# Parking part of Wq between the rows of a zero tile, and moving half of the backward stores to another queue

## The chip, the cores and the metric

The kernel runs on one core of a Trainium2 chip. A core has a matrix engine (TensorE, PE in the profile; PEld is its weight load), VectorE (DVE), ScalarE (ACT), GpSimd (POOL) and SyncE (SP). Transfers between the chip's memory and the on-chip buffer (SBUF, 128 partitions) are issued from SP, POOL or ACT and are carried out by 16 DMA engines. The metric is the device time of one execution in microseconds, as the median of several runs.

## The reference, cut to what matters

One token (448 numbers) goes through a pre-norm attention layer over a sliding window of 4096 cached keys and values, and through a gated bilinear layer. The function returns the output and the gradients of every input but one:

```python
    W = min(4096, max(256, Sk // 4))            # 4096 of Sk = 32768
    q = (x @ wq).reshape(B, Sq, Hq, Dh)...      # 16 heads of 256
    k = jnp.repeat(k_cache[:, :, Sk - W:, :], rep, axis=1)
    v = jnp.repeat(v_cache[:, :, Sk - W:, :], rep, axis=1)
    p = _softmax(jnp.einsum("bhqd,bhkd->bhqk", q, k) * (Dh ** -0.5), axis=-1)
    o = jnp.einsum("bhqk,bhkd->bhqd", p, v)
...
    h = x + _A_ref(_layernorm(x), ...)
    h2 = h + _B_ref(_layernorm(h), ...)
    _out, _vjp = jax.vjp(_f, A_x, A_k_cache, A_v_cache, A_wq, A_wo, B_w_gate, B_w_up, B_w_down)
    return (_out, *_vjp(grad_out))
```

The gradients of the two caches (`out_2` for K, `out_3` for V) have the caches' full shape, 8 heads x 32768 x 256 in bf16. Only the last 4096 positions of each head are computed; the other 28672 are zeros that the kernel must write: 16 regions of 14.7 MB each. Together with the rest the kernel writes 280.6 MB and reads 49.2 MB.

## The kernel before

**Zeros.** The tile `zeros` has 128 partitions of 8192 bf16 numbers (16 KB each). Partitions 32 to 95 are set to zero at the start. A fill (`fill`, L81) reads 16 of them, every fourth from 32 to 92 (`ALL`), again and again into a region of `out_2` or `out_3`. SP's queue (`FILL`) issues 15 whole regions and part of the last one, one after the other (L86 to L104). What is left of the last region is dealt out in small pieces on POOL's queue (`deal_rest`, `lap` 0 in the middle and `lap` 1 at the very end), some partitions with more than others. Partitions 0 to 31 and 96 to 127 of `zeros` hold something else from the forward pass on: quarters of the moments (`quarter`, L124). The 48 partitions between the fills' rows (33 to 35, 37 to 39 and so on) are zero and are read by nothing.

**Wq.** The weight of 448 x 4096 is laid out as 128 partitions of 14336 numbers: seven blocks of `HQ` = 2048, called i = 0 to 6. It is loaded twice. At the start SP loads all but the first `KW` = 896 columns into the big buffer `BIG` (L68), and ScalarE's queue loads those 896 into a place where they stay (`wq_kept`, L69). The buffer's slots are then used for V. For the gradient of x, in the backward loop, POOL loads Wq again (`dxn_load`, L653, blocks 0 to 3 after step 2 and 4 to 6 after step 3 of the loop) and VectorE multiplies each block with dq and sums it up (`wq_product`, L657; `dxn_part`, L661).

**Forward.** q is made by 112 small matmuls (L306). Then, for each of the 8 heads of K and V, PE transposes K (L341), forms the scores, VectorE scales K by the softmax (L394) and PE forms moments (L398 to L404). POOL's queue (`IO`) loads K, V and all later weights in an order that is written out by hand (`io_load`, each issued after the one before). A feed-forward part with its own gradients follows.

**Backward loop.** Eight steps s (L757), one for each head. In each, 32 matmuls (L764) make the rows of the gradients of K and V, which ScalarE and VectorE copy in turn out of PSUM into a pair of slots of `BIG` (`evac`, L289). When a step's 32 rows are there, POOL's queue stores the two halves of the pair, 2 MB each (L788). Which slots a step uses stands in `PAIR`; a slot can be written again when its store has landed. VectorE also works at jobs for the other gradients in between (`during`, L693: `o4_job` to `o8_job` are outer products that are stored from POOL's queue, `dxn_part` the second use of Wq, `dx_out` the gradient of x).

Waits between engines are semaphores that the tile framework sets. It has eight for transfers issued from SP and ACT together, used in turn, and eight for those from POOL; a transfer that takes a semaphore waits until the transfer that had it eight before has landed.

Of the kernel before, what the change touches and what calls it, by code (L numbers as in the profile page):

```python
# [42 lines left out]
def kernel(  # L43
# [23 lines left out]
    for c0, c1 in ((KW, 4 * HQ), (4 * HQ, NI * HQ)):  # L67
        FILL.dma_start(out=wq_sb[:, c0:c1], in_=flat_rows(A_wq)[:, c0:c1])  # L68
    S_.dma_start(out=wq_kept, in_=flat_rows(A_wq)[:, 0:KW])  # L69
# [4 lines left out]

    zeros = const.tile([128, ZW], bf16)
    for p in (32, 64):
        V_.memset(zeros[p:p + 32, :], 0.0)
    def region(o, g):
        return o[0, g, 0:Sk - W, :].rearrange("s d -> (s d)")

    def fill(eng, flat, rows, n, f):  # L81
        p = len(range(128)[rows])
        eng.dma_start(out=flat.rearrange("(p n f) -> p n f", p=p, f=f), in_=zeros[rows, 0:f].unsqueeze(1).to_broadcast([p, n, f]))

    ALL = slice(32, 93, 4)
    for g in range(G):  # L86
        for o in (out_2, out_3):
            if (g, o) != (G - 1, out_3):
                fill(FILL, region(o, g), ALL, 8 * NZ, ZW)
# [12 lines left out]
    deal(FILL, 0, 3, 14)  # L102
    deal_all(24, ZW)
    deal_all(8, 1224)  # L104
# [68 lines left out]


# [4 lines left out]
    ones_f = const.tile([128, 128], f32)  # L179
    V_.memset(ones_f[:], 1.0)  # L180
# [106 lines left out]
    evac_ctr = [0]  # L287

    def evac(out, in_):  # L289
        if evac_ctr[0] % 2 == 0:  # L290
            S_.copy(out=out, in_=in_)  # L291
        else:
            V_.tensor_copy(out=out, in_=in_)  # L293
# [10 lines left out]
    for b in range(16):  # L304
        for i in range(NI):
            P_.matmul(q_ps[:, :, b], lhsT=wq_at(i, b * 128, 128), rhs=xx1[:, i, :], start=(i == 0), stop=(i == NI - 1))  # L306
# [341 lines left out]
    wq2 = [slot(3 + i // 4)[:, (i % 4) * HQ:(i % 4 + 1) * HQ] for i in range(NI)]  # L648

    def wq_from(i):  # L650
        return 0 if i else KW

    def dxn_load(i0, i1):  # L653
        c = wq_from(i0)
        IO.dma_start(out=slot(3 + i0 // 4)[:, c:(i1 - i0) * HQ], in_=flat_rows(A_wq)[:, i0 * HQ + c:i1 * HQ])

    def wq_product(w, i, c, n):  # L657
        V_.tensor_tensor_reduce(out=w, in0=w, in1=dq_bc[:, i % 2, c:HQ] if c else dq_bc[:, i % 2, 0:w.shape[-1]], scale=1.0, scalar=0.0,  # L658
                                op0=ALU.mult, op1=ALU.add, accum_out=Pq[:, n:n + 1])

    def dxn_part(i0, i1):  # L661
        if i0 == 0:
            wq_product(wq_kept, 0, 0, NI)
            yield
        for i in range(i0, i1):
# [156 lines left out]
```

## Time and profile before

| | us |
|---|---|
| median of 3 runs (778.31 to 779.84) | 778.7 |
| the profiled execution | 779.32 |
| its span, first to last instruction | 777.5 |
| DVE busy in the span | 402.0 (52%) |
| PE busy | 468.0 (60%) |
| ACT busy | 177.1 (23%) |
| POOL busy | 43.3 (6%) |

The span is what the views of the trace divide into stretches; the profiled execution's own time is 1.8 us longer. Of the 330.4 MB that were moved, SP's queue (q1) moved 230.9 MB, POOL's (q0) 98.6 MB and ScalarE's (q10) 0.2 MB. A row of the costliest groups names line, engine, operation and tiles, then the busy time and the mean of one in ns, then the idle time before and what ended it. A row of DMA issues names tiles, queue and count, the size of one in KB and the median time from issue to landing. The chain of waits is followed back from the last instruction.

### The profile page before, as it was taken

The numbers are of one execution on the slowest core, as the hardware profiler recorded it, in microseconds if no ns is written. First come the engines' busy times: TensorE is split into PE (matmuls) and PEld (weight loads), VectorE is DVE, ScalarE is ACT, GpSimd is POOL, SyncE is SP. The second block draws the span as 40 slices with busy tenths as digits, with TensorE's granted clock in tenths as the row PEclk, the third lists the DMA queues.
The fourth block names the chain that finished last, engine by engine and source line by source line (L and its number), as shares of the span: only waits on it lengthen the run. The fifth ranks groups of instructions, "written<-read, shape, count | busy, mean of one in ns | idle before, by whom it ended". The sixth has DMA issues, their size and how long they took to land.

```text
span 777.5 us, 10855 instructions
## 1 busy us (share of the span) xinstructions
PE 468.0 (60%) x4375; PEld 257.5 (33%) x4420; DVE 402.0 (52%) x1179; ACT 177.1 (23%) x278; POOL 43.3 (6%) x88
## 2 busy tenths in 40 slices
PE   4798898899899612234076998980957598200000
PEld 3654554565555311113052443430333232000000
DVE  5477677677667311255954656667577377200000
ACT  0322322321120000034333444440413244100000
POOL 3000000000000000010000001000001010100000
PEclk9998998999999855555555555555555555555555
DMA  9999999999999999999999999999999999999998
GB/s 363 427 425 428 426 425 430 428 426 428 424 428 429 429 430 430 433 430 430 424 428 430 430 429 430 428 427 431 428 430 429 429 427 431 430 433 432 428 429 349
DMA packets 25683, 330.44 MB, mean 425 GB/s; under 512 B 3069, under 2 KB 3199, under 8 KB 5046
## 3 DMA queue, kind: packets, MB, share of 16 engines
q1 hardware_dynamic: 14557, 230.94, 69.6%
q0 software_dynamic: 10928, 98.59, 30.1%
q8 instruction: 34, 0.56, 0.3%
q10 hardware_dynamic: 148, 0.23, 0.1%
q14 instruction: 16, 0.12, 0.0%
HBM read 49.15 MB, written 280.59 MB: 424 GB/s over the span
## 4 chain that ended last, share of the span: by engine, by line
PE 40%; DMA 28%; DVE 13%; issue 4%; ACT 2%; another core or an unknown queue 2%; POOL 0%; POOLq 0%; DVEq 0%; ACTq 0%
PE MT L398 12%; DMA out_dram<-BIG 10%; PE tr L341 8%; PE d_ps L764 7%; DMA BIG<-in_B_w_down_dram 7%; DMA BIG<-in_A_wq_dram 6%; DMA BIG<-in_A_k_cache_dram 4%; DVE BIG L588 2%; PE sT L346 2%; DMA BIG<-in_A_wo_dram 2%; DVE BIG L574 1%; PE dp L346 1%; DVE zeros L415 1%; ACT BIG L291 1%
## 5 line engine op out<-in xcount | busy, mean ns | idle before, releaser
L764 PE MATMUL d_ps<-BIG 32*128 32x512 bf16 x256 | 121.8, 607 | 41.3 <-ACT BIG L291 23.9
L398 PE MATMUL MT<-BIG 128*128 128x512 bf16 x467 | 140.4, 409 | 2.1 <-DVE BIG L394 0.4
L394 DVE TENSOR_SCALAR BIG<-BIG,pf 128x256 bf16<-128x256 bf16 x512 | 114.3, 282 | 29.0 <-PE MT L398 26.0
L291 ACT CAST BIG<-d_ps 128x512 bf16<-128x512 f32 x156 | 88.9, 587 | 154.9 <-PE d_ps L764 121.6
L341 PE MATMUL tr<-ident_bf,BIG 128*128 128x128 bf16 x1024 | 113.1, 268 | 14.7 <-DVE doW L588 12.6
L341 PEld LDWEIGHTS <-BIG 128*128 128x128 bf16 x1024 | 80.8, 120 | 43.4 <-issue 41.4
L293 DVE COPY BIG<-tr 128x1024 bf16<-128x1024 bf16 x92 | 63.3, 688 | 43.6 <-PE tr L341 43.3
L293 DVE CAST BIG<-d_ps 128x512 bf16<-128x512 f32 x100 | 68.0, 684 | 16.5 <-DMA out_dram<-BIG 8.2
L291 ACT COPY BIG<-tr 128x1024 bf16<-128x1024 bf16 x36 | 36.4, 1012 | 127.8 <-PE tr L341 120.5
L346 PEld LDWEIGHTS <-BIG 128*128 128x128 bf16 x1024 | 37.4, 102 | 80.1 <-DVE BIG L293 53.3
L401 PEld LDWEIGHTS <-BIG 128*128 128x128 bf16 x512 | 42.2, 99 | 52.9 <-issue 16.9
L401 PE MATMUL acc<-pT_all,BIG 128*128 128x2 bf16 x512 | 45.0, 164 | 16.6 <-DVE kbar L420 15.0
L398 PEld LDWEIGHTS <-BIG 128*128 128x128 bf16 x512 | 40.5, 103 | 23.8 <-issue 16.8
L404 PE MATMUL acc<-pT_all,BIG 128*128 128x2 bf16 x512 | 44.3, 164 | 0.0
L764 PEld LDWEIGHTS <-BIG 32*128 32x128 bf16 x256 | 21.3, 113 | 65.9 <-issue 46.4
L346 PE MATMUL dp<-doT,BIG 128*128 128x2 bf16 x512 | 24.4, 168 | 12.2 <-DVE BIG L293 11.4
L521 DVE CUSTOM_DVE_ANT_0 dh_bc<-BIG,dh_bc 128x448 bf16<-128x448 bf16 x14 | 8.7, 624 | 44.1 <-DMA BIG<-in_B_w_down_dram 43.8
L404 PEld LDWEIGHTS <-BIG 128*128 128x128 bf16 x512 | 30.1, 96 | 0.9
L542 PE MATMUL y<-BIG,hh_bf 128*1 128x448 bf16 x14 | 5.9, 565 | 29.7 <-DMA BIG<-in_B_w_down_dram 29.0
L346 PE MATMUL sT<-qT,BIG 128*128 128x2 bf16 x512 | 22.3, 165 | 0.8 <-ACT BIG L291 0.6
L658 DVE CUSTOM_DVE_ANT_0 BIG<-BIG,Mt 128x2048 bf16<-128x2048 bf16 (+2 forms) x8 | 16.1, 2017 | 8.0 <-DMA BIG<-in_A_wq_dram 7.1
L745 DVE TENSOR_TENSOR BIG<-r_ps,mrow 96x1024 bf16<-96x1024 bf16 (+2 forms) x15 | 18.3, 1221 | 1.4 <-PE r_ps L750 1.1
(186 smaller groups left out, 369.1 us busy)
## 6 DMA issues: line engine op xcount, KB each, us to landing
out_dram<-zeros SPq DMA_DIRECT2D x15, 14336.0 KB, 146.7
out_dram<-BIG POOLq DMA_DIRECT2D x16, 2048.0 KB, 42.7
BIG<-in_A_v_cache_dram POOLq DMA_DIRECT2D x8, 2048.0 KB, 23.5
BIG<-in_A_k_cache_dram POOLq DMA_DIRECT2D x12, 1024.0 KB, 14.7
out_dram<-zeros SPq DMA_DIRECT2D x1, 6144.0 KB
out_dram<-BIG POOLq DMA_DIRECT2D x6, 896.0 KB, 39.0
BIG<-in_A_k_cache_dram POOLq DMA_DIRECT2D x2, 2048.0 KB, 25.4
out_dram<-zeros POOLq DMA_DIRECT2D x2, 1680.0 KB, 77.9
```

Source lines behind the costliest of these rows:

```text
L291: S_.copy(out=out, in_=in_)
L293: V_.tensor_copy(out=out, in_=in_)
L341: P_.transpose(tr[:, i, dh, :], x_at(g, 4 * q + i)[:, dh * 128:(dh + 1) * 128], ident_bf[:])
L346: P_.matmul(out_ps[:, 4 * q + i, :], lhsT=xt[:, i, dh, :], rhs=vecT[:, 4 * g + dh:4 * g + dh + 3:2], start=(dh == 0), stop=(dh == 1))
L394: V_.tensor_scalar(out=pk[:, i, h, :], in0=K[:, t, :], scalar1=pf[:, t, h:h + 1], scalar2=None, op0=ALU.mult)
L398: P_.matmul(MT[hf][:], lhsT=v_at(g, t)[:, hf * 128:(hf + 1) * 128], rhs=pk[:, i, :, :].rearrange("p h d -> p (h d)"), start=(t == 0), stop ...
L401: P_.matmul(acc[:, 2 * hf:2 * hf + 2], lhsT=v_at(g, t)[:, hf * 128:(hf + 1) * 128], rhs=pT_all[:, g, t, :], start=(t == 0 and hf == 0), st ...
L404: mm = P_.matmul(acc[:, 4 + dk:7 + dk:2], lhsT=K[:, t, dk * 128:(dk + 1) * 128], rhs=pT_all[:, g, t, :], start=False, stop=(t == T - 1), s ...
L588: V_.tensor_tensor_reduce(out=wg_sb[:, 0:D], in0=parked.get(b, wo_b(b)), in1=dh_bc[:], scale=1.0, scalar=0.0, op0=ALU.mult, op1=ALU.add, a ...
L658: V_.tensor_tensor_reduce(out=w, in0=w, in1=dq_bc[:, i % 2, c:HQ] if c else dq_bc[:, i % 2, 0:w.shape[-1]], scale=1.0, scalar=0.0, op0=ALU ...
L745: V_.tensor_tensor(out=rows[p0:p1], in0=r_ps[p0:p1, :].unsqueeze(1).to_broadcast([p1 - p0, 8, 128]), in1=mrow[p0:p1, :].unsqueeze(2).to_br ...
L764: mm = P_.matmul(d_ps[:].rearrange("p w d -> p (w d)"), lhsT=rows[32 * k:32 * k + 32, a, :], rhs=R[32 * k:32 * k + 32, :], start=True, sto ...
```

## The change

Blocks 3 to 6 of Wq (columns `ZQ` = 6144 to 14336, 16 KB in each partition) are handled by partition. In the 48 partitions of `zeros` between the fills' rows they are loaded into `zeros` at the start and stay there. In the other 80 partitions they are loaded into `BIG` as before, and loaded again in the backward loop. The q product takes both: the seven blocks from `BIG`, in which the 48 rows are set to zero, and four more blocks from `zeros`, in which all other rows are zero; for this ScalarE zeroes partitions 0 to 31 and 96 to 127 at the start. The second use of these blocks is split too: on all 128 partitions from the loaded slot (`dxn_part`), and for the 48 rows from `zeros` (`dxn_rows`, 32 partitions at a time, all rows of each) into `Pz`; a mask (`kept_row`) then picks `Pz` for the 48 rows.

Half of the stores of the backward loop (the gradients of V, `out_3`) are issued from ScalarE's queue. SP's fills are no longer all issued ahead in the program: ten first, one after every second step, the rest at the end, then the deals of SP. The jobs of the loop stand in a new order. Three orderings are added for the scheduler: copies out of PSUM behind the last store on ScalarE, a job's instruction behind the last copy of VectorE, and fills and stores of SP and ScalarE one behind the other. The last are orderings of the program without a semaphore between the two engines.

```diff
-    for c0, c1 in ((KW, 4 * HQ), (4 * HQ, NI * HQ)):
-        FILL.dma_start(out=wq_sb[:, c0:c1], in_=flat_rows(A_wq)[:, c0:c1])
-    S_.dma_start(out=wq_kept, in_=flat_rows(A_wq)[:, 0:KW])
+    wq_d = flat_rows(A_wq)
+    ZQ = (NI - 4) * HQ
+    for rows, c0, c1 in ((slice(0, 128), KW, ZQ), (slice(0, 32), ZQ, NI * HQ), (slice(96, 128), ZQ, NI * HQ)):
+        FILL.dma_start(out=wq_sb[rows, c0:c1], in_=wq_d[rows, c0:c1])
+    S_.dma_start(out=wq_kept, in_=wq_d[:, 0:KW])
...
     for p in (32, 64):
         V_.memset(zeros[p:p + 32, :], 0.0)
+    for p in (0, 96):
+        S_.activation(out=zeros[p:p + 32, :].bitcast(f32), in_=ones_f[p:p + 32, 0:1].to_broadcast([32, ZW // 2]), func=ACT.Copy, scale=0.0)
+    for r in range(1, 4):
+        FILL.dma_start(out=zeros[32 + r:96:4, :], in_=wq_d[32 + r:96:4, ZQ:NI * HQ])
...
-    for g in range(G):
-        for o in (out_2, out_3):
-            if (g, o) != (G - 1, out_3):
-                fill(FILL, region(o, g), ALL, 8 * NZ, ZW)
+    regions = [region(o, g) for g in range(G) for o in (out_2, out_3)][:-1]
+    filled = [None]
+
+    def next_fills(n):
+        for _ in range(n):
...
+                with tc.issue_after(filled[0].ins):
+                    filled[0] = fill(FILL, regions.pop(0), ALL, 8 * NZ, ZW)
+
+    next_fills(10)
...
-    deal(FILL, 0, 3, 14)
-    deal_all(24, ZW)
-    deal_all(8, 1224)
+    def deal_fill():
+        with tc.issue_after(filled[0].ins):
+            deal(FILL, 0, 3, 14)
+            deal_all(24, ZW)
+            deal_all(8, 1224)
...
+    def load_wq_rest(dst):
+        IO.dma_start(out=dst[32:96:4, :], in_=wq_d[32:96:4, ZQ:NI * HQ])
+
+    for p in (32, 64):
+        nc.gpsimd.memset(wq_sb[p:p + 32, ZQ:NI * HQ].bitcast(u32), 0.0)
+    load_wq_rest(wq_sb[:, ZQ:NI * HQ])
...
-            P_.matmul(q_ps[:, :, b], lhsT=wq_at(i, b * 128, 128), rhs=xx1[:, i, :], start=(i == 0), stop=(i == NI - 1))
+            P_.matmul(q_ps[:, :, b], lhsT=wq_at(i, b * 128, 128), rhs=xx1[:, i, :], start=(i == 0), stop=False)
+        for i in range(4):
+            P_.matmul(q_ps[:, :, b], lhsT=zeros[:, i * HQ + b * 128:i * HQ + (b + 1) * 128], rhs=xx1[:, NI - 4 + i, :],
+                      start=False, stop=(i == 3))
...
+    def dxn_load(part):
+        if part == 0:
+            IO.dma_start(out=slot(3)[:, KW:ZQ], in_=wq_d[:, KW:ZQ])
+            return
+        for r in range(4):
+            for p in (r, 96 + r):
+                IO.dma_start(out=slot(4)[p:p + 29:4, :], in_=wq_d[p:p + 29:4, ZQ:NI * HQ])
+        load_wq_rest(slot(4))
...
+    def dxn_rows(p):
+        for i in range(4):
+            wq_product(slot(3)[p:p + 32, ZQ:SLOT], zeros[p:p + 32, i * HQ:(i + 1) * HQ], dq_bc[p:p + 32, (NI - 4 + i) % 2, :], Pz[p:p + 32, i:i + 1])
             yield
...
+        V_.copy_predicated(out=Pq[:, 3:NI], mask=kept_row[:, 0:1].to_broadcast([128, 4]).bitcast(u32), data=Pz[:])
...
-        3: [o5_job(half(2, 0), 0), o5_job(half(2, 1), 8), dxn_part(0, 4)],
-        4: [o5_job(half(3, 0), 16), o5_job(half(3, 1), 24), dxn_part(4, 7), dx_out()],
-        5: [o8_job(half(2, 0), 0), o8_job(half(2, 1), 7), o4_job(half(4, 0), 0), o4_job(half(4, 1), 2)],
-        6: [o4_job(half(3, 0), 4), o4_job(half(3, 1), 6)],
+        3: [o5_job(half(2, 0), 0), o5_job(half(2, 1), 8), dxn_part(0)],
+        4: [o5_job(half(3, 0), 16), o4_job(half(3, 1), 6), dxn_part(1)],
+        5: [o8_job(half(2, 0), 0), o8_job(half(2, 1), 7), dxn_rows(32), o4_job(half(4, 0), 0)],
+        6: [o5_job(half(4, 1), 24), o4_job(half(3, 0), 4), dxn_rows(64)],
+        7: [dx_out(), o4_job(half(2, 0), 2)],
...
-            evac(pair[:, :, t, :], d_ps[:])
+            if stored is None:
+                evac(pair[:, :, t, :], d_ps[:])
+            else:
+                with tc.issue_after(stored.ins):
+                    evac(pair[:, :, t, :], d_ps[:])
...
-        for w, o in ((0, out_3), (1, out_2)):
-            tail = IO.dma_start(out=o[0, g, Sk - W:, :].rearrange("(p t) d -> p t d", t=T), in_=pair[:, w])
+        for w, o, eng in ((0, out_3, S_), (1, out_2, IO)):
+            tail = eng.dma_start(out=o[0, g, Sk - W:, :].rearrange("(p t) d -> p t d", t=T), in_=pair[:, w])
+            if eng is S_:
+                tc.add_manual_dep(tail.ins, filled[0].ins.name, mybir.DependencyInfo(mybir.DependencyClass.NoSync, mybir.DependencyReason.DATA), reason="order")
+                stored = tail
+        if s % 2 == 0:
+            next_fills(1)
+            tc.add_manual_dep(filled[0].ins, stored.ins.name, mybir.DependencyInfo(mybir.DependencyClass.NoSync, mybir.DependencyReason.DATA), reason="order")
+    next_fills(len(regions))
+    deal_fill()
     with tc.issue_after(tail.ins):
         deal_rest(1)
```

In the built program SP issues three loads of Wq, three loads into `zeros`, fifteen fills and three deals; ScalarE issues its three early loads and eight stores; POOL issues nine loads (eight of 8 partitions, one of 16) in place of the second reload, and eight stores fewer.

## The prediction

> **What bounds the kernel now.** I read the strip of 40 slices first, then the DMA queues, then stretches of the end, the issues with their landings, and last the chain of waits.
>
> ```profile
> PE   4798898899899612234076998980957598200000
> DMA  9999999999999999999999999999999999999998
> GB/s 363 427 425 428 426 425 430 428 426 428 424 428 429 429 430 430 433 430 430 424 428 430 430 429 430 428 427 431 428 430 429 429 427 431 430 433 432 428 429 349
> q1 hardware_dynamic: 14557, 230.94, 69.6%
> q0 software_dynamic: 10928, 98.59, 30.1%
> ```
>
> The DMA row never drops, while the matmuls end some five slices before the end. q1 is SP's queue (zero fills), q0 POOL's (loads and stores); a third, q10, is ScalarE's and carried 0.23 MB. The stretches (length, busy time of PE, PEld, DVE, ACT, POOL, clock, DMA share, GB/s) say it sharper:
>
> ```profile
> 0.00:20.00 20.00, 8.47 (x42) 8.24 (x43) 11.59 (x29) 1.54 (x2) 6.00 (x20) 1.00 0.92 365
> 20.00:40.00 20.00, 14.82 (x269) 12.63 (x268) 8.74 (x46) 5.98 (x9) 0.00 (x0) 1.00 1.00 425
> 700.00:773.00 73.00, 0.00 (x0) 0.00 (x0) 0.00 (x0) 0.00 (x0) 0.00 (x0) 0.50 1.01 429
> 773.00:777.50 4.50, 0.00 (x0) 0.00 (x0) 0.00 (x0) 0.00 (x0) 0.00 (x0) 0.50 0.26 105
> ```
>
> From 700 to 773 no engine computes and the transfers still run at 429 GB/s. So bytes set the end, and compute has a margin. The chain of waits names matmuls for 40% of the span; that is the compute chain, not the bound. How wide the margin is, POOL's last issues show (start, length, count, idle before):
>
> ```profile
> 666.50 1.05 POOL L788 DMA_DIRECT2D out_dram<-BIG  x2 [14.16 <-issue]
> 667.92 0.58 POOL L83 DMA_DIRECT2D out_dram<-zeros  x1 [0.36 <-DMA out_dram<-BIG]
> ...
> 692.80 0.63 POOL L83 DMA_DIRECT2D out_dram<-zeros  x1 [6.12 <-DMA out_dram<-BIG]
> ```
>
> The last two stores go out at 666.5. They and the last zero deals are 4.2 + 2.6 = 6.8 MB, 16 us at 429 GB/s. To be through by 775 with some 5 us for issues they could leave as late as 754, 87 us later than they do; the four deals wait for older stores (26 us from 667 to 693), all or none of which may remain, so the margin lies between 61 and 87 us; I take 70.
>
> **The change, part by part.**
> (1) Bytes. The second load of Wq leaves out 48 partitions x 16,384 B = 0.786 MB. q1's row gives 0.696 x 16 x 777.5 / 230.94 = 37.5 engine-us per MB, over 16 engines 2.34 us per MB: **-1.84 us**. It is on the bound, so it counts in full if the eight new loads of eight partitions spread evenly: 5 rows of 16 KB an engine instead of 8. If they all fell on eight engines, those would hold 1 + 8 = 9 rows, one more than before, and the -1.84 becomes +0.6.
> (2) Queue of eight stores (2048 KB each, 16.8 MB) from q0 to q10. q0's row gives 38.0 engine-us per MB against 37.5, which over 16.8 MB and 16 engines is 0.5 us; q0's figure holds smaller packets too. Bounds -0.5 and 0; I take -0.2.
> (3) First load. Before, 128 partitions at a time; now two loads of 32 partitions (0.52 MB each), three of 16 into the zero tile and one of 16 from POOL. No row shows a load into 32 neighbouring partitions. Bounds: no loss, or twice the time for 1.05 MB, +2.5 us. The nearest rows are those of the first 20 us, DMA at 0.92 with POOL's five 2 MB loads there to use what stands idle; I take +0.3, near no loss. [...]
> (4) POOL work: eight more issues at 0.53 us (L655's length) and two memsets of 32x4096, by VectorE's same memset (L77, 3.47 us) some 7 us. Hidden: POOL waits most of the time, and what follows them waits for V anyway. One more thing is late, though. POOL's fifth load among the DMA issues (KB, us to landing), and q's matmuls in the chain of waits (start, length):
>
> ```profile
> BIG<-in_A_v_cache_dram POOLq DMA_DIRECT2D x1, 2048.0 KB, 55.6
> ```
>
> ```profile
> 22.64 3.12 PE q_ps L306 x112
> ```
>
> The last 16 partitions of Wq are loaded behind this V (issued 3.57, landed 59.2) on the same queue, and q needs them, as do the first copies out of PSUM, which wait for the same semaphore. So q starts at about 61 instead of 22.6: the compute chain slips 38 us. The 64 extra matmuls (64 x 3.12/112 = 1.8 us) and ScalarE's two zero fills of 32x4096 (3.6 us each, L585's row) come on top of nothing: the fills run in that wait.
> (5) VectorE: eight products 32x2048, by the 128x2048 form 2282 ns each, and one masked copy: 18.3 us in steps 5 and 6 of the backward loop. Slip so far 38 + 2 + 18 = 58 us, inside the 70. Behind them on VectorE stand the copies out of PSUM, and behind those PE; nothing of it reaches the transfers' end.
> (6) Given back: the second wq load had 47.8 us to land at 519.6 because POOL's queue was full of stores; with half of them gone from that queue it should be 20 to 30 us. I leave this 0 to -25 us out.
> (7) The stores on ScalarE. ScalarE's issue waits for VectorE's last copy of the pair; behind it stand ScalarE's own copies for the next step, which needed that step's factors anyway. Issue itself 0.36 us (L69, 128 partitions), 8 x 0.36 = 3 us, hidden in the margin. Their semaphores are shared with the fills, eight in turn: store 0 needs the third fill done, store 6 the eleventh, each long past. So 0, if ScalarE's issue is taken at once.
> (8) Fills: same bytes on SP; the first deal (42 x 16 KB, 0.69 MB) moves from before the fills to behind them. The other way round, fill 14 now waits for store 1, and the last deals for stores 3 and 4; with SP's queue two fills deep and those stores out by 580, SP is not yet there. 0.
> Sum: -1.84 - 0.2 + 0.3 = **-1.7 us** on the profiled span of 777.5 (that execution took 779.3, 1.8 outside the span; the median of the runs is 778.7): 775.8 span, **777.0** by the median. With the bounds of (1) to (3) and 1 us for how evenly the 16 engines run dry (773 to 777.5): 775.4 to 780.
>
> **Rivals.**
> A, held issue (slower). SP's fills are not taken at once, by the instructions that use the zero tile (ns of an issue: shortest, median, longest); ScalarE's early load was, by its timeline:
>
> ```profile
> L83 SPq DMA_DIRECT2D out_dram<-zeros x18: 608/47490/60944, 5.2 to 708.8; - x18
> ```
>
> ```profile
> 1.56 0.36 ACTq L69 DMA_DIRECT2D BIG<-in_A_wq_dram  x1
> ```
>
> Median 47.5 us an issue (608 ns the shortest): SP stands before a full queue all along. If ScalarE's issue has to pass the same place, store 0, ready at 446 + 38 = 484, waits for the fill in front, and ScalarE's PSUM copies, PE's four buffers and the step with it. While fills last, a step then takes about one fill, 52 us: stores 0 to 3 end at 484 + 4 x 52 = 692. The other four steps took 666.5 - 536.7 = 130 us before, 90 without waits for full queues, plus 18 of (5): last stores at 800 to 840, plus 16 for the rest: 816 to 856; if only half of the stores meet a fill, about 795. Price: 20 to 80 us, likely 830. For it: 47.5 us. Against it: L69 was taken in 0.36 us with two loads of SP under way, but then SP's queue was not full. It decides from a mean hold of (70 - 58)/8, 1.5 us, if (6) gives nothing, and 4.6 if it gives 25.
> [...]
> B, late chain without held issues: with three queues at work POOL's share falls from a half to a third, its loads land later and the slip is 90 instead of 58: end 776 + 90 - 70 = 796. For it: POOL's stores already took 42.7 us to land; against: half as many are left.
> C, nothing visible: the loss of (3) at its bound, or uneven loads of (1), eats the bytes: 778.7 - 1.84 - 0.2 + 2.5 = 779.2.
> D, the change doesn't do what it says, the reload is not shorter: the reload loads 80 rows of 128, so this is out but for the uneven spread in C.
>
> **How the numbers follow.** Measurement of this kernel can tell about 0.2%, 1.6 us, from no change. Forecast (bytes gone, no stall, 775.4 to 778.3) 0.43; C (778 to 780) 0.13; A 0.33; B 0.11. Of the forecast's 0.43 some 0.36 lies under 777.1, the rest within 0.2%; C is within 0.2% but for 0.03. So faster 0.36, same 0.17, slower 0.33 + 0.11 + 0.03 = 0.47. Slower is more likely than faster, by two mechanisms; the likeliest single outcome is 777.0. Its own range is 775.4 to 780. To leave out no more than 0.2 the range has to take in B and the lower part of A: 775.4 to 840.
>
> **What would show it.** Right: q0 and q10 sum 0.8 MB less in reads, DMA share 1.0 to about 771, ScalarE's store issues under 1 us, q's first matmul near 61, last stores near 700 to 725. A: ScalarE's issues of L833 lasting tens of us, DMA slices below 9 after 740. B: those issues short and the last stores after 736. C: a dip in the first 20 us below 365 GB/s, or a longer tail than 4.5 us. Wrong in the main: no compute left after 725, DMA full to the end, and still no gain.

## The result, and the profile after

| | before | after |
|---|---|---|
| median of 5 runs, us | 778.67 | 786.22 |
| lowest to highest | 778.31 to 779.84 | 785.90 to 787.57 |
| ratio, 95% interval | | 1.0099 [1.0084, 1.0114] |
| span of the profiled execution | 777.5 | 785.8 |

The changed kernel is 7.5 us slower. Its profiled execution took 787.57 us, the slowest of its five; time and span differ by 1.8 us in every execution. The page after, with the strip of 40 slices and the DMA queues:

```profile
PE   3105889889899996122240869988930768876000
DMA  9999999999999999999999999999999999999995
GB/s 264 418 433 429 427 428 425 430 425 427 430 422 429 428 427 430 430 430 430 431 428 430 424 430 431 430 429 430 429 430 430 428 431 430 426 433 430 431 428 232
q1 hardware_dynamic: 14605, 230.67, 69.0%
q0 software_dynamic: 9952, 81.29, 25.0%
q10 hardware_dynamic: 1300, 17.01, 5.1%
HBM read 48.37 MB, written 280.59 MB: 419 GB/s over the span
```

The saving is there: 48.37 MB are read instead of 49.15, and half of the stores are in q10. The transfers still fill the span. The strip differs at its two ends: the first slice ran at 363 GB/s before and runs at 264, the last at 349 and now 232. The stretches of the changed kernel (length, busy time of PE, PEld, DVE, ACT, POOL, granted clock, DMA share, GB/s):

```profile
0.00:20.00 20.00, 7.28 (x30) 6.89 (x30) 12.50 (x23) 9.79 (x4) 13.70 (x23) 1.00 0.93 265
20.00:40.00 20.00, 2.33 (x19) 2.16 (x19) 3.55 (x30) 0.26 (x1) 0.00 (x0) 1.00 1.00 420
700.00:773.00 73.00, 18.43 (x84) 7.59 (x82) 19.32 (x37) 10.02 (x18) 4.61 (x8) 0.52 1.01 428
```

In the first 20 us the DMA share is 0.93 as before (0.92), with 365 - 265 = 100 GB/s less, 2.0 MB: the engines are as busy and move less. In the trace's packet records from 6 to 18 us a packet of 16 KB takes a mean of 1.05 us in POOL's queue and 1.09 in SP's, where POOL's before had a mean of 0.67 and a median of 0.61; ScalarE's packets of 1.8 KB take 0.13 instead of 0.07. The end, in stretches:

```profile
773.00:776.00 3.00, 0.00 (x0) 0.00 (x0) 0.00 (x0) 0.00 (x0) 0.00 (x0) 0.50 0.74 312
776.00:779.00 3.00, 0.00 (x0) 0.00 (x0) 0.00 (x0) 0.00 (x0) 0.00 (x0) 0.50 0.48 201
779.00:782.00 3.00, 0.00 (x0) 0.00 (x0) 0.00 (x0) 0.00 (x0) 0.00 (x0) 0.50 0.18 70
782.00:785.80 3.80, 0.00 (x0) 0.00 (x0) 0.00 (x0) 0.00 (x0) 0.00 (x0) 0.50 0.00 0
```

A share of 0.48 from 776 to 779 I read as half of the engines done and half not: of the sixteen landings of the last transfer eight come by 776.5 us and eight from 778.6 to 781.9. After 782 nothing moves, and the program still takes 3.8 us to end. The timeline shows what was issued last (start, length, count, idle before):

```profile
725.36 0.34 ACTq L833 DMA_DIRECT2D out_dram<-BIG  x1
725.84 0.56 POOL L833 DMA_DIRECT2D out_dram<-BIG  x1 [9.83 <-issue]
726.42 2.48 POOL L92 DMA_DIRECT2D out_dram<-zeros  x4
```

The last four fills of POOL went out at 726 to 729 us; before, the last of them went out at 692.8. They landed at 756, 781.3, 781.5 and 781.9 us (before: the last at 770.9). SP's last fill landed at 781.87 (before 776.58).

**Where 8.3 us of span come from.** Fewer bytes: -1.84. The start: by 30 us packets with 9.49 MB have begun instead of 11.54, and 2.05 MB at 0.427 MB a us are +4.8. Uneven engines: a transfer leaves sixteen landings in the trace, which I read as one for each engine. Those of the transfer that lands last have a mean of 777.3 and a maximum of 781.9, 4.6 apart, against 774.5 and 776.6, 2.0 apart: +2.6. (The DMA shares above give the same mean: 773 + 3 x (0.74 + 0.48 + 0.18) = 777.2.) The close, from the last landing to the end: 3.9 instead of 1.0, +2.9. Sum 8.5. This is a reading of two traces; the experiments had to show that each term is real, and what causes it. The start's term is that of one execution. The traces of six experiments below have the same loads at the start, and they are 1.0 to 2.2 MB behind the kernel before at 30 us, 2.4 to 5.1 us.

### The profile page after: what moved, and what is told of

The parts are those of the page before. It is cut to its first block, busy times and chain, and to the rows that moved or that the text cites. A ratio compares the mean times of both kernels' runs of the same rounds, so it can differ in the third digit from the quotient of the medians.

```text
span 785.8 us, 11038 instructions
## 1 busy us (share of the span) xinstructions
PE 473.2 (60%) x4484; PEld 261.0 (33%) x4484; DVE 424.7 (54%) x1198; ACT 184.6 (23%) x281; POOL 50.7 (6%) x91
## 2 busy tenths in 40 slices
DMA packets 25908, 329.68 MB, mean 420 GB/s; under 512 B 3340, under 2 KB 3470, under 8 KB 5317
## 3 DMA queue, kind: packets, MB, share of 16 engines
HBM read 48.37 MB, written 280.59 MB: 419 GB/s over the span
## 4 chain that ended last, share of the span: by engine, by line
PE 47%; DVE 19%; DMA 16%; another core or an unknown queue 5%; issue 3%; ACT 3%; POOL 0%; POOLq 0%; DVEq 0%; ACTq 0%
PE MT L424 14%; PE d_ps L804 10%; PE tr L367 10%; DMA BIG<-in_B_w_down_dram 6%; DVE BIG L316 4%; DMA out_dram<-BIG 3%; DMA BIG<-in_A_wq_dram 3%; DVE BIG L614 2%; DVE BIG L689 2%; PE sT L372 2%; DMA BIG<-in_A_k_cache_dram 2%; ACT BIG L314 2%; DVE BIG L784 2%; DMA BIG<-in_A_wo_dram 1%
## 5 line engine op out<-in xcount | busy, mean ns | idle before, releaser
L367 PE MATMUL tr<-ident_bf,BIG 128*128 128x128 bf16 x1024 | 116.0, 269 | 54.6 <-ACT BIG L314 41.3
L424 PE MATMUL MT<-BIG 128*128 128x512 bf16 x512 | 148.5, 406 | 0.0
L804 PE MATMUL d_ps<-BIG 32*128 32x512 bf16 x256 | 119.9, 602 | 34.5 <-DVE BIG L784 16.7
L316 DVE CAST BIG<-d_ps 128x512 bf16<-128x512 f32 x100 | 68.3, 687 | 17.4 <-PE d_ps L804 16.5
L172 POOL DMA_DIRECT2D BIG<-in_A_k_cache_dram x13 | 6.9, 533 | 228.8 <-PE acc L430 130.7
```

Of the source, the lines that this page charges most:

```text
L316: last_copy[0] = V_.tensor_copy(out=out, in_=in_)
L367: P_.transpose(tr[:, i, dh, :], x_at(g, 4 * q + i)[:, dh * 128:(dh + 1) * 128], ident_bf[:])
L424: P_.matmul(MT[hf][:], lhsT=v_at(g, t)[:, hf * 128:(hf + 1) * 128], rhs=pk[:, i, :, :].rearrange("p h d -> p (h d)"), start=(t == 0), stop ...
L804: mm = P_.matmul(d_ps[:].rearrange("p w d -> p (w d)"), lhsT=rows[32 * k:32 * k + 32, a, :], rhs=R[32 * k:32 * k + 32, :], start=True, sto ...
```

## The experiments

Each was run beside the kernel before on the same chip, and its ratio is to that. The chips differ between experiments (the kernel before took 778.5 to 779.9 us on them), so a difference of some tenths of a us between two variants means little, and where it matters the ratios are compared too.

**1. The start alone, in the kernel before.** Its second load of Wq is cut into 32 neighbouring partitions (first run) and into every fourth partition (second run):

```diff
-FILL.dma_start(out=wq_sb[:, c0:c1], in_=flat_rows(A_wq)[:, c0:c1])
+rows = slice(p, p + 32)      # first: p = 0, 32, 64, 96
+rows = slice(r, 128, 4)      # second: r = 0, 1, 2, 3
+FILL.dma_start(out=wq_sb[rows, c0:c1], in_=flat_rows(A_wq)[rows, c0:c1])
```

> The kernel before, with one edit: its second load of Wq (columns 4*HQ to 7*HQ, 128 partitions) becomes four loads of 32 neighbouring partitions each, the same bytes in the same queue. Theory P (loads of 32 neighbouring partitions are what slowed the changed kernel's start, and they slow every queue while they run): the rate between 6 and 18 us falls from about 400 GB/s to 250 to 300, packets of 16 KB on POOL's loads take 1.0 us instead of 0.61, and since the transfers fill the rest of the span the kernel ends 3 to 6 us later, 782 to 785 us. Rival (the slow start comes from something else in the change, such as the 16-row loads into the zero tile or the later start of the fills): the start stays at about 400 GB/s and the time at 778.7 us, within 0.5.

> The kernel before, with its second load of Wq as four loads of 32 partitions again, but every fourth partition (r, r+4, ...) instead of 32 neighbours; bytes, queue and number of loads as in the run that was 5.5 us slower. Theory P (32 neighbouring partitions share too few ways into SBUF, and their packets hold up everyone's): packets of 16 KB stay at 0.61 us in the first 20 us and the time stays at 778.7 us, within 0.7. Rival (four small loads are slow because they are small, or because a queue with more loads starts its packets later): the time rises by about 5 us again, to 784.

784.15 us, 1.0068 [1.0052, 1.0085], and 779.33 us, 0.9995 [0.9986, 1.0004]. The stretches of the first and then of the second (before: 413 and 413 GB/s from 6 to 18 us, 393 to 24):

```profile
6.00:12.00 6.00, 1.94 (x9) 1.94 (x9) 4.95 (x10) 0.00 (x0) 1.09 (x4) 1.00 1.02 372
12.00:18.00 6.00, 5.10 (x22) 4.87 (x22) 2.29 (x13) 0.00 (x0) 0.00 (x0) 1.00 1.09 308
18.00:24.00 6.00, 3.09 (x24) 2.60 (x24) 4.03 (x31) 1.27 (x2) 0.00 (x0) 1.00 0.96 244
```

```profile
6.00:12.00 6.00, 1.94 (x9) 1.94 (x9) 4.95 (x10) 0.00 (x0) 1.09 (x4) 1.00 0.98 410
12.00:18.00 6.00, 5.10 (x22) 4.87 (x22) 2.29 (x13) 0.00 (x0) 0.00 (x0) 1.00 1.01 425
18.00:24.00 6.00, 4.07 (x68) 3.71 (x69) 4.02 (x31) 1.27 (x2) 0.00 (x0) 1.00 0.99 339
```

The same four loads and bytes, and a share of about 1 in both: 32 neighbours cost 5.5 us, 32 partitions spread over all 128 nothing. Theory P's slow packets are there and "many small loads" is out. Its sizes came out milder and longer than written: from 6 to 18 us POOL's 16 KB packets take a mean of 0.82 us in the first run (1.0 was expected) and 0.62 in the second, and the rate is lowest only after 18 us. Why neighbours are slow, neither run shows; theory P's shared ways into SBUF are a guess.

**2. The start of the changed kernel.** First all small loads go and VectorE fills the zero tile's rows from the landed Wq (product with a mask); then only the two loads of 32 neighbours go, and the loads into the zero tile stay:

```diff
 # first run: no small load, no ScalarE zeroing, q from Wq alone
+for c0, c1 in ((KW, 4 * HQ), (4 * HQ, NI * HQ)):
+    FILL.dma_start(out=wq_sb[:, c0:c1], in_=wq_d[:, c0:c1])
+V_.tensor_scalar(out=zeros[p:p + 32, :], in0=wq_sb[p:p + 32, ZQ:NI * HQ], scalar1=kept_row[p:p + 32, 0:1], scalar2=0.0, op0=ALU.mult, op1=ALU.add)
 # second run; POOL's late load, its memsets and the second part of the q product go too
-for rows, c0, c1 in ((slice(0, 128), KW, ZQ), (slice(0, 32), ZQ, NI * HQ), (slice(96, 128), ZQ, NI * HQ)):
+for rows, c0, c1 in ((slice(0, 128), KW, ZQ), (slice(0, 128), ZQ, NI * HQ)):
```

> The changed kernel, with the loads of Wq at the start as they were before (128 partitions, all rows), so that no load of 32 or 16 partitions is left in the start; the kept rows get into the zero tile by a product of the landed Wq with a mask on VectorE, and the first product uses Wq alone, as before. It loads 0.79 MB more than the changed kernel at the start, and as much as the kernel before; the reload keeps its eight small loads. The fills start when the mask product is done, a few us later than before. Theory P (the 32-partition loads cost the start 4.8 us): the rate between 6 and 18 us is back at about 400 GB/s, and the time falls by 4.8 us less what 0.79 MB cost at 0.42 MB a us, 1.9, so by some 3 us, to 783.3 us. Rival (the start is slow for another reason, or what is lost there is hidden by the engines' uneven ends): the time stays at 786.2 or rises by the 1.9 us of bytes, to 788.

> The changed kernel, with its two start loads of 32 neighbouring partitions replaced by one of all 128; the three loads of every fourth partition into the zero tile stay, the late load of 16 rows on POOL's queue goes, as do POOL's two memsets and the product's second part. It moves 0.79 MB more than the changed kernel, 1.84 us. Theory P (the two loads of 32 neighbours alone slow the start): the first 20 us move as many bytes as before the change, 7.3 MB instead of 5.3, the first product no longer waits for POOL's late load, so the compute ends some 35 to 40 us sooner, POOL's last fills land by 760, and the time is 786.2 - 4.8 + 1.84 - 2.9 = 780.3 us. Rival (the loads into the zero tile are to blame as well): the first 20 us stay at 5.3 to 6.5 MB, and the time is 783 us or more.

778.72 us, 0.9995 [0.9986, 1.0005], and 782.05 us, 1.0037 [1.0024, 1.0049]. One line each, the first 20 us of the first run and of the second:

```profile
0.00:20.00 20.00, 7.87 (x32) 7.39 (x32) 6.45 (x32) 1.54 (x2) 6.24 (x20) 1.00 0.92 379
```

```profile
0.00:20.00 20.00, 8.49 (x42) 8.27 (x43) 11.60 (x30) 10.05 (x5) 6.00 (x20) 1.00 0.93 380
```

The first gained 7.5 us where 3 were expected. Part of the miss is that the expectation subtracted 1.9 us of bytes which that kernel doesn't move (329.66 MB, like the changed kernel's 329.68). The rest is the end: without the late load on POOL's queue its compute runs 41 us earlier, POOL's last fills go out at 688 and land by 754, the landings are 3.2 us apart instead of 4.6, and the program ends 1.0 us after the last. 4.8 + 1.4 + 2.9 = 9.1 is the difference of the spans (785.8 to 776.7). The second came 1.8 us above its forecast, between theory P and its rival. Its span is 3.7 us longer than the first run's: 1.84 are the 0.79 MB that it moves more, 1.0 the spread of its last landings (4.2 us between mean and maximum instead of 3.2), 0.5 its close, and 0.4 the start, where by 40 us packets with 15.66 MB have begun instead of 15.85. So the loads of 32 neighbours make nearly all of the start's loss, and those into the zero tile at most 0.4 us.

**3. Which engines the reload uses.** If the eight reload transfers of eight rows all load the same eight engines (theory E), those end late, and giving them less of the dealt fills helps. The dealt fills are redistributed, the sum kept; `deal(IO, 0, 4, 24)` gives 24 units to each of four rows from row 0 on. The first try had fills of one row; the others keep 2 to 7 rows. "Low" takes four units of 16 KB from each of the rows dealt as 0 to 6 and gives four more to 9 to 15, "high" does the reverse:

```diff
-deal(IO, 0, 4, 24); deal(IO, 4, 3, 6);  deal(IO, 7, 2, 38); deal(IO, 9, 7, 15)
+deal(IO, 0, 4, 20); deal(IO, 4, 3, 2);  deal(IO, 7, 1, 34); deal(IO, 8, 1, 42); deal(IO, 9, 7, 19)   # first try
+deal(IO, 0, 4, 20); deal(IO, 4, 3, 2);  deal(IO, 7, 2, 38); deal(IO, 9, 7, 19)   # low
+deal(IO, 0, 4, 28); deal(IO, 4, 3, 10); deal(IO, 7, 2, 38); deal(IO, 9, 7, 11)   # high
```

> The changed kernel, with the last uneven fills dealt anew: four units of ZW fewer on each of engines 0 to 7 and four more on 8 to 15, the sum the same. Theory E (the reload's eight loads of eight partitions all fall on the same eight engines, which then end 4 to 5 us after the others): either the two halves of the engines now end together and the time falls by 2 to 2.5 us, to 783.7 to 784.2 us, or, if the eight late engines are the other half, the gap doubles and the time rises by 2 to 2.5 us to about 788.5. Which of the two it is tells the half. Rival (the engines' ends differ by chance of the queues, not by these loads): the time stays at 786.2, within 0.7, and the spread of the ends stays at about 5 us without changing its halves.

> The kernel with the product in place of the small loads at the start (778.7 us), with the uneven fills of POOL's queue dealt anew: 20, 2, 38 and 19 units instead of 24, 6, 38 and 15 to the engines 0 to 3, 4 to 6, 7 and 8, 9 to 15. No fill has a single row this time. Theory E (the reload's eight loads of eight rows all go through engines 0 to 7, and end these late): the last fill's sixteen landings, now in two groups 5 us apart, draw together, and the time falls by 1 to 1.5 us, to 777.4 us. If the eight late engines are 8 to 15, the gap grows to 10 us and the time rises by about 2.4 us, to 781. Rival (the two groups don't come from the eight loads): the groups stay and the time stays within 0.5.

> The same, dealt the other way: 28, 10, 38 and 11 units. Theory E with the late engines among 0 to 7: the gap grows to 10 us and the time rises by 2.4 us, to 781; with the late engines among 8 to 15: it closes and the time falls to 777.4 us. One of this pair must be faster than 778.7 and the other slower, or theory E falls.

> The changed kernel, with the dealing that relieves engines 0 to 6 by four units each and gives them to 9 to 15, in fills of 2 to 7 rows as before, without any fill of a single row. Theory E: the two groups of the last landings, 775 and 780 us, draw together, and the time falls by 2 to 2.4 us, to about 784. Rival (in the changed kernel the late engines are late for another reason than in its variant with the product): the time stays at 786.2 within 0.7. The first try of this, with fills of one row of 34 and 42 units, took 824 us: if the single rows were its fault, nothing of that is left here; if the new deal was, this run is as slow.

The first try took 824.28 us, 1.0579 [1.0553, 1.0605], and told nothing of the engines (experiment 6). On the variant with the product (778.72), low took 777.09 us, 0.997 [0.9958, 0.9982], and high 781.2 us, 1.0019 [1.001, 1.0028]; on the changed kernel low took 783.98 us, 1.007 [1.0056, 1.0084], 2.2 less. In all three the sign is theory E's, and the time is within 0.3 us of what was written. (By the ratios, low gains 1.9 us on the variant and high costs 1.9; by the times, 1.6 and 2.5.) The end of the variant as it was, then low, then high:

```profile
768.00:772.00 4.00, 0.00 (x0) 0.00 (x0) 0.00 (x0) 0.00 (x0) 0.00 (x0) 0.50 0.69 292
772.00:776.70 4.70, 0.00 (x0) 0.00 (x0) 0.00 (x0) 0.00 (x0) 0.00 (x0) 0.50 0.28 117
```

```profile
768.00:772.00 4.00, 0.00 (x0) 0.00 (x0) 0.00 (x0) 0.00 (x0) 0.00 (x0) 0.50 0.85 359
772.00:775.36 3.36, 0.00 (x0) 0.00 (x0) 0.00 (x0) 0.00 (x0) 0.00 (x0) 0.50 0.14 55
```

```profile
768.00:772.00 4.00, 0.00 (x0) 0.00 (x0) 0.00 (x0) 0.00 (x0) 0.00 (x0) 0.50 0.54 232
772.00:776.00 4.00, 0.00 (x0) 0.00 (x0) 0.00 (x0) 0.00 (x0) 0.00 (x0) 0.50 0.46 196
776.00:779.80 3.80, 0.00 (x0) 0.00 (x0) 0.00 (x0) 0.00 (x0) 0.00 (x0) 0.50 0.13 50
```

In the high run the share stays near one half for 8 us (0.54, then 0.46), which I read as one group of engines that has run dry. The last landings' mean and maximum are 3.2 us apart in the variant, 1.9 in low (772.4 and 774.4) and 6.3 in high. The changed kernel's trace shows the cause itself: the sixteen landings of the reload's eight transfers fall into two groups of eight. From one transfer to the next the first group comes 1.22 us later and the second 1.83, so the gap grows by 0.61 us each time, to 4.7 us at the eighth; a packet of 16 KB takes 0.61 us in POOL's queue meanwhile. I read it as all eight transfers putting their rows on the same eight engines. Since low helps and high costs, these are, at least for the most part, those that the dealing counts as 0 to 7. The variant with low is faster than the kernel before by 0.3%; the low dealing alone, in the kernel before, was not run.

**4. The queue alone.** Both stores of a step back on POOL's queue and all fills issued at the start, in the variant with the product; and the queue part of the change alone, in the kernel before:

```diff
 # first run
-for w, o, eng in ((0, out_3, S_), (1, out_2, IO)):
+for w, o, eng in ((0, out_3, IO), (1, out_2, IO)):
-next_fills(10)
+next_fills(15)
 # second run, in the kernel before
-for w, o in ((0, out_3), (1, out_2)):
+for w, o, eng in ((0, out_3, S_), (1, out_2, IO)):
```

> The kernel with the product in place of the small loads at the start (778.7 us), with all backward stores back on POOL's queue and all fills issued at the start, as in the kernel before, so that only the saved reload is left of the change. Theory Q (the move of the queue is worth nothing, since the DMA engines are full either way and the compute ends 40 us ahead of them): 778.7 us within 0.7, with POOL's stores landing 42 us after their issue again instead of 24. Rival R (the quicker stores and the quicker reload hold the end): the stores and the reload are late, the compute ends 15 to 30 us later than the 727 of the changed kernel, and from an end of 760 on the time rises, to 781 or more.

> The kernel before, with the queue part of the change alone: half of the backward stores on ScalarE's queue, six of the fills issued in between. All bytes as before. Theory Q2 (the queue is worth time only where POOL's queue would end last; before the change its last landing is 5.7 us ahead of SP's): 778.7 us within 0.5, POOL's stores landing 24 us after their issue instead of 43. Rival (quicker stores help the end in any kernel, as the 2.7 us between the last two variants may suggest): 776 to 777 us. Rival A of the prediction (ScalarE's issues are held by a full queue): 782 us or more.

781.4 us, 1.0024 [1.0014, 1.0034], 2.7 above its base, and 779.27 us, 1.0003 [0.9994, 1.0012], no difference. The source line of the stores in the second (durations in ns: shortest, median, longest; first and last start):

```profile
L803 POOL DMA_DIRECT2D out_dram<-BIG x8: 531/531/533, 443.0 to 712.4; - x8
L803 ACTq DMA_DIRECT2D out_dram<-BIG x8: 338/338/377, 447.1 to 712.0; - x8
```

ScalarE's issues take 0.34 us, and nothing holds them, though SP's take tens of us (a median of 47.5 for its fills in the kernel before, 39.5 in the changed one). Alone, the move gains nothing. In the variant it is worth 2.7 us (2.3 by the ratios), and theory Q falls there: the compute ends as early (ScalarE's last copy starts at 682.5 us, and at 683.5 in the base), but with sixteen stores on POOL's queue the last dealt fill goes out at 717.7 instead of 687.6 and lands at 775.5, and the span ends at 779.65, 4.15 us later. Rival R named a late compute, which isn't seen. That points to the close.

**5. The close.** Two runs put the changed kernel's last dealt fills earlier on POOL's queue, a third adds the low dealing to that, and a fourth gives these fills to ScalarE instead:

```diff
-with tc.issue_after(tail.ins):        # behind the last step's stores
-    deal_rest(1)
+if s == 6:                            # first run; second and third: s == 5
+    with tc.issue_after(tail.ins):
+        deal_rest(1)
 # third run: the low dealing besides; fourth run, in deal_rest(1): deal(S_, ...) for deal(IO, ...)
```

> The changed kernel, with the last fills of POOL's queue issued one group earlier, so that POOL's queue is empty before SP's and a transfer of SP's queue is the last to land. Theory L (after POOL's last transfer lands, POOL and the close of the program take 3 to 4 us more, after SP's last one about 1 us): the time falls by 2.5 to 3 us, to about 783.4 us, with the same landing of the last byte, near 782. Rival (what is seen after the last landing is the close of the program whichever queue ends it): the time stays at 786.2 within 0.7 and the span still ends 3 to 4 us after the last landing.

> The changed kernel, with POOL's last four fills issued two groups of stores earlier (after the sixth instead of the eighth), so that they land near 735 us and the two POOL stores behind them near 745 to 760. Theory L2 (end = POOL's last landing + 3.9 us or SP's + 1 us, whichever is later): SP's last landing near 781 ends the run 1 us later, and the time falls by 2 to 3 us, to 783.2 to 784.2 us. Rival (about 4 us after the last landing whichever queue it is, or the stores held up behind the fills make the compute later): 786 us or more.

> The run with POOL's last fills two groups earlier, and the dealing that took the changed kernel to 784.0 us besides. If the two losses are separate and add up: 786.2 - 2.3 - 2.5 = 781.4 us, and what is left against 778.7 is the start's loss of 4.8 less the saved bytes, 1.84: 781.6. If they are one loss told twice: 783.5 to 784 us.

> The changed kernel, with the four last uneven fills (two of them small) issued by ScalarE instead of POOL, at the same place; bytes and rows the same. Theory L2 (the program ends 3.9 us after the last landing in POOL's own queue, or 1 us after the last in SP's, whichever is later; the run that moved these fills one group earlier couldn't show it, since its last POOL store still landed at 778.9 us, 3.9 us before its end): POOL's last landing is now its store's, near 755 us, the end follows SP's last landing, near 782, by about 1 us, and the time falls by 2 to 3 us, to 783.2 to 784.2. Rival (3 to 4 us after the last landing, whichever queue it belongs to): the time stays at 786.2 within 0.7.

785.64 us, 1.0089 [1.0074, 1.0104]; 786.58, 1.0103 [1.0089, 1.0116]; 784.22, 1.0069 [1.0056, 1.0083]; 809.85, 1.04 [1.0386, 1.0414]. None of the four came out as theory L2 or the adding up of losses had it, and the first three didn't move POOL's end away: the stores behind the early fills now waited for them, and POOL's last landing stayed at 778.9, 780.4 and 778.9 us. The third came out at 784.2 where two separate losses would have given 781.4; since POOL's end is as late as before, it doesn't tell whether they are separate. In the fourth the scheduler issued the fills between 5 and 78 us instead of at the end, and engines ended as late as 806.8. Its DMA share is 0.21 from 780 to 800 us and 0.08 from there on. 806.8 is 24.9 us above the 781.9 of the changed kernel, which is some 41 packets of 16 KB at 0.61 us one after the other, an estimate; which engines end so late, and why, isn't shown. What the traces did show is a pattern (us from their landings):

```
kernel                           POOL's last  SP's last  end     after POOL's  after SP's
before                           770.93       776.58     777.55  6.62          0.97
product in place of small loads  754.25       775.71     776.69  22.4          0.98
the same, low dealing            756.25       774.37     775.36  19.1          0.99
changed kernel                   781.94       781.87     785.80  3.86          3.93
changed, fills one step earlier  778.92       780.58     782.78  3.86          2.20
changed, fills two steps earlier 780.38       780.56     784.24  3.86          3.68
changed, low dealing             777.46       777.21     781.32  3.86          4.11
product, all stores on POOL      775.50       775.98     779.65  4.15          3.67
```

In these eight the end is 1.0 us after SP's last landing or about 3.9 after POOL's, whichever is later. (In the run with the queue part alone it isn't quite so: POOL lands at 773.37, SP at 775.97, and the end is 776.94, 3.6 after POOL's.) The last experiment sets that alone: in the fastest variant, POOL issues the last even fills instead of SP.

```diff
 def deal_all(n, f):
-    fill(FILL, last[used[0]:used[0] + 16 * n * f], ALL, n, f)
+    fill(IO, last[used[0]:used[0] + 16 * n * f], ALL, n, f)   # called at the end of deal_rest(1)
```

> The fastest variant so far (777.1 us: product in place of the small start loads, dealing that relieves engines 0 to 6), with its two last even fills (24 units and 8 short ones on all sixteen rows, 6.6 MB) issued by POOL at the very end instead of SP. Bytes and rows are the same. Theory L2 (the program ends 3.9 us after POOL's last landing, or 1 us after SP's): POOL's landing is now the last, near 774.4 us, the span ends 3.9 us later instead of 1.0, and the time rises by 2.9 us, to 780.0. Rival (the close is as long after any queue): 777.1 us within 0.7, and the end 1 us after the last landing.

779.7 us, 1.0008 [0.9999, 1.0017], 2.6 above its base. The last landing is where it was (774.2 us, 774.4 in the base), and the end comes 2.5 us later. At the end of the program SP's closing steps come first behind its transfers and then behind POOL's longest step: in the changed kernel from 782.3 us, where SP's last landing is at 781.87, and to 785.3, where POOL's step ends at 785.0. The rows of the closing steps of POOL and SP (ns: shortest, median, longest; first and last start), of the changed kernel, of the fastest variant, and of that variant with POOL's fills at the end:

```profile
L870 POOLq DRAIN  x3: 46/102/56957, 728.1 to 785.5; - x3
L870 SPq DRAIN  x3: 7/7/13, 782.3 to 785.3; - x3
```

```profile
L861 POOLq DRAIN  x3: 46/102/69852, 689.4 to 775.1; - x3
L861 SPq DRAIN  x3: 7/7/13, 774.5 to 774.8; - x3
```

```profile
L860 POOLq DRAIN  x3: 46/102/74970, 702.1 to 777.6; - x3
L860 SPq DRAIN  x3: 7/7/13, 774.5 to 777.3; - x3
```

SP gets through its own waits at 774.5 us in both variants. Where POOL's queue ended early, the last step follows 0.3 us later; where POOL's last transfer landed at 773.9, it follows 2.8 us later, as in the changed kernel (3.0). That is the third term, and it is POOL's. POOL's longest DRAIN, a closing step, starts at its last issue and ends at 728.1 + 57.0 = 785.0, at 759.3 and at 777.0 us, each time 3.0 to 3.1 us after POOL's last landing; where that is early, as in the second, it costs nothing. Over all runs this time is 2.7 to 3.4 us, and where POOL is last the program ends 0.8 us behind it. What POOL does within the DRAIN the trace doesn't show.

**6. The fills of a single row**, alone, in the kernel before:

```diff
-deal(IO, 7, 2, 38)
+deal(IO, 7, 1, 38)
+deal(IO, 8, 1, 38)
```

> The kernel before, with one uneven fill of two rows (38 units each, engines 7 and 8) split into two fills of one row and 38 units each; bytes and rows the same. Theory S (a fill of a single row doesn't go through one engine: it is cut up over all of them, which then read one partition together and slow every queue, as in the first dealing experiment): 16 KB packets take longer than 0.61 us between 380 and 440 us, the rate falls below 300 GB/s there, the engines end unevenly, and the time rises by 20 to 40 us, to 800 to 820. Rival (that experiment was slow because its new deal sent the units elsewhere): 778.7 us within 1.

819.96 us, 1.0531 [1.0511, 1.0552]: the same bytes and rows, 41 us more. From 360 to 400 us:

```profile
360.00:380.00 20.00, 7.34 (x39) 7.18 (x40) 12.46 (x39) 10.38 (x4) 0.00 (x0) 0.50 1.02 225
380.00:400.00 20.00, 9.18 (x130) 6.84 (x128) 13.52 (x46) 3.35 (x5) 1.12 (x2) 0.50 0.97 254
```

The slow time starts at 360, not 380 as written, but it is the same sign as at the start: a full share at half the rate. The large packets of POOL's queue take a mean of 1.8 to 2.9 us from 360 to 390, SP's 0.70 to 0.81. In these 30 us POOL's queue moved 2.10 MB with 60.7% of the sixteen engines' time; in the kernel before it moved 2.12 MB with 17.4%. The last landings then spread over 39 us. So the single rows were at fault in the first dealing try, and their packets held far more than one engine each. That such a fill is cut over all engines, as theory S put it, isn't shown.

## Why the prediction was wrong

The four effects: 778.7 - 1.84 (bytes) + 4.8 (start, experiments 1 and 2) + 2.2 (dealing, experiment 3) + 2.6 (close, experiment 5) = 786.5, against 786.2 measured. That it comes so near is partly luck, since the start's 4.8 stands for 2.4 to 5.1; the bytes had no run of their own. The prediction's likeliest outcome was 777.0, and it failed by three terms that it had at or near nothing: the start, the uneven engines and the close.

- **(3), the first load, is the step that failed most.** It took +0.3 with a bound of +2.5 and measured +4.8. The bound, 1.05 MB at twice their time, was an estimate; no run shows that factor. The runs showed that while such loads are under way the packets of all queues are slow (16 KB take 1.05 us in POOL's queue and 1.09 in SP's; 0.82 in POOL's in experiment 1), so 2 MB were lost, not 1. Of "nearest rows" there were none: rows of loads over 128 partitions say nothing about 32 neighbours. With the bound itself and the -0.2 of (2) the sum is -1.84 - 0.2 + 2.5 = +0.5: the right sign, and still too small.
- **(1), bytes**: right in the -1.84. That the eight reload transfers might all fall on the same eight engines stood there as a bound, 2.4 us worse. By the landings it is what happened, and the runs put 1.6 to 2.5 on it.
- **(4) and the margin**: the late q was right. The chain of waits of the changed kernel (start, length, what) goes through it, with the first copy out of PSUM at 63 us where 61 was forecast:

```profile
21.63 41.59 another core or an unknown queue
63.30 1.02 ACT BIG L314
```

- The slip was right as well: the last stores went out at 725.4 and 725.8 us instead of 666.5, 59 us later where (4) and (5) made 58. The last dealt fill slipped by 35.4 (692.8 to 728.2), since it no longer waited for older stores. The margin of 61 to 87 us failed. It gave POOL's last 6.8 MB the whole rate, 16 us; but the last fill took 54 us from issue to landing, and in that time POOL's queue moved 5.6 MB and SP's 13.1. It also left out the close. The queue alone pushed that fill to 714.8 us at no cost (experiment 4), and a push to 717.7 in the variant cost 2.7 us. As far as two kernels can be compared, the margin of the fill was some 22 to 25 us.
- **(2), (7), (8)**: the queue is worth nothing by itself, and ScalarE's issues take 0.34 to 0.38 us. Right.
- **(5)** eight products at 2282 ns, as forecast. **(6)** the reload's last load lands 14.5 us after its issue and the first 31.7, about as hoped; but the last stores slipped by the full 59 us, so none of that came back at the end.
- **Rival A**, with 0.33, is refuted: none of ScalarE's eight issues took over 0.38 us. **Rival B** had a late chain right and its price wrong: nothing waited, the lateness went through POOL's last fills into 2.6 us of close. **Rival C** had both of the other mechanisms, but as one or the other, at 779.2; they came together, and (3) at up to twice its bound. Its signs came true: 265 GB/s in the first 20 us, and a tail of 12.8 us behind 773. The close stood in none of the rivals. That slower had the larger chance, 0.47, was luck: 0.44 of it were A and B, and neither mechanism is what made the kernel slower.

With the small start loads replaced and the uneven engines mended, the change gives about what its bytes are worth: 777.09 us, 1.6 less than before by the times and 2.3 by the ratio.

## What to carry to other kernels

Where transfers fill the span, cost a load by the partitions it covers and by what it does to every other queue's packets while it runs, not by its own bytes, and try a part of the partitions spread over all 128: four loads of 32 neighbours cost 5.5 us here, the same bytes with every fourth partition nothing. Look how far the engines run dry together before counting a saving of bytes: here transfers of eight rows decided that, and with 1.9 us between mean and maximum of the last landings instead of 3.2 the variant gained 1.6 to 1.9 us. Follow each queue to its own last landing and the close behind it (3.9 us behind POOL's here, 1.0 behind SP's) before calling a compute chain's margin wide.

## What the runs showed of the hardware that was not expected

- While loads into 32 neighbouring partitions ran, they slowed the packets of every queue. In the changed kernel POOL's of 16 KB took a mean of 1.05 us (0.67 before), SP's 1.09, and ScalarE's of 1.8 KB 0.13 (0.07 before); in experiment 1 POOL's took 0.82, and 0.62 where every fourth partition was loaded.
- Eight transfers of eight rows, issued by POOL one after the other, landed from 598.5 to 611.5 us, some 1.8 us apart. Eight of the sixteen landings of each came 1.22 us after those of the one before and eight 1.83 us, which I read as the same eight engines every time.
- Where POOL's queue was last, the program ended 3.9 us after its last landing (3.86 in five runs, 3.91 and 4.15 in two); elsewhere 1.0 to 1.5 us after SP's. In every run POOL's closing DRAIN ended 2.7 to 3.4 us after that landing, so the figure isn't fixed.
- Two fills of one row in place of one of two rows cost 41 us.
